# A list of 2,766 steps written anew: the issue order of a fused mLSTM and rational feed-forward kernel

## The chip, the cores and the metric

One core of a Trainium2 chip runs the whole program. The time is device time in microseconds (us) of one execution, and the profile shows the instructions of one such execution on the five engines: PE (TensorE), DVE (VectorE), ACT (ScalarE), POOL (GpSimd) and SP (SyncE), which here issues nearly all transfers. PEld is PE's weight load, which runs beside its matmuls.

## The reference

What is computed, cut to what matters (B=4, H=8, S=768, D=40; the feed-forward has 320 inputs, 2048 hidden columns and 3072 tokens):

```python
for t in range(S):                       # mLSTM, for every batch b and head h
    m_new = np.maximum(f_gate[:, :, t] + m, i_gate[:, :, t])
    f_stab = np.exp(f_gate[:, :, t] + m - m_new)
    i_stab = np.exp(i_gate[:, :, t] - m_new)
    m = m_new
    C = f_stab[..., None, None] * C + i_stab[..., None, None] * np.einsum('bhd,bhe->bhde', vt, kt)
    n = f_stab[..., None] * n + i_stab[..., None] * kt
    h_tilde = np.einsum('bhde,bhe->bhd', C, qt)
    denom = np.maximum(np.abs(np.einsum('bhd,bhd->bh', n, qt)[:, :, None]), 1.0)
    y[:, :, t] = sigmoid(o_gate[:, :, t]) * h_tilde / denom

x = y.transpose(0, 2, 1, 3).reshape(B * S, H * D)
h = x @ w_in
P = a[0] + a[1] * h + a[2] * h**2 + a[3] * h**3
Q = 1.0 + abs(b[0]) * abs(h) + abs(b[1]) * h**2
out = (P / (Q + 1e-06)) @ w_out
```

## The kernel before

The recurrence is worked in 24 units (`attention`, L841): a unit is 128 time steps of one batch with its 8 heads. Two units make a pair (`outputs`, L1056), whose result is 256 tokens of feed-forward input. The feed-forward (`feed_forward`, L1196) takes the tokens in 12 blocks of 256, and each block in 8 steps of 256 hidden columns, so there are 96 steps, named by block and step (`f2_0_3` is block 0, step 3). The weights arrive as raw 64-bit words and are split once, at the start, into a high and a low part (`split64`, L729), in 18 pieces: `i0` to `i7` and `j0`, `j1` of w_in, `o0` to `o7` of w_out.

Nothing is scheduled when the program is built. Every piece of work is put into a plan with its engine and with what it reads and writes (`_Plan.add`, L66), and the string `ORDER` (L145) then lists all steps by name, in one sequence for all engines and for the SP queue. `listed` (L89) reads it and `issue` (L114) issues the steps in that sequence. Each engine runs its own steps strictly in that order (`_Queue`, L22, ties each instruction to the one before it on its queue, and its line 34 is the one that nearly all instructions show in the profile). A buffer is handed out when its step is issued, so the order also decides which work waits for which buffer. A step's dot is its count: `s1_o7.1` is the second half of `s1_o7`.

The names that the order and the prediction use:

- Gates. `early` (L490) is the chain on DVE that makes the gate terms of the first 256 time steps; its last three steps on DVE are `early.17` (the exponentials, tile g), `early.20` and `early.21` (a scan that makes the running products a). `gate.5` to `gate.25` (`gates`, L565) do the same for the other 512 time steps, with four subtractions `lx` on DVE and four `li` on POOL; their tile is gate_x.
- Weight pieces. `raw` is the load; `s0`, `s2` and `o0` run on ACT, `s1` (tiles lo0, lo1) and `s3` (tile z) on DVE, `o2` (tiles wi, wo, wY) on POOL.
- Units. `pf`, `pa`, `tk`, `tq`, `S`, `ow` on PE (tiles fb, pa, kq, kq, ps, ow), `sc` (a scan, tile e), `qa`, `P`, `u0`, `u1` on DVE, `kp`, `ke`, `d0`, `d1` on POOL, `ek`, `eq` on ACT. Pairs: `it`, `i1` and the transpose `xt` on PE (tiles y, px), `rc`, `x`, `xl` on DVE (tiles na, xn, xk), `ab`, `xh` on ACT, `g` on POOL. `og` is the sigmoid of the output gate on ACT, which needs another activation table than `y`.
- A feed-forward step. `f1` on PE (16 matmuls into ph, in two halves), `ha`, `p1`, `u` on ACT, `p3` on DVE, `w` on POOL, `y`, `r0` on ACT, `gh` on DVE (tile gH), `f2` on PE (8 matmuls from gH into po), `m` on DVE (w<-w,gH), `rm` on POOL (p<-p,w), `gl` on DVE (tile gL), `f3` on PE (4 matmuls from gL). The last step, 11_7, is done in two halves.
- `hot` (90, at the start) and `hz` (24, at the end) are matmuls without use, which keep PE's clock up.

Of the kernel before, what the change touches and what calls it, by code (L numbers as in the profile page):

```python
# [150 lines left out]
s1_i0 o0_o1 tk_0 ek_0 raw_i6 s0_o5 s2_o5 s3_i4 o2_o1 s3_i0 li o0_i4 lx.1 lk_1 gate.3 s0_o7.1 lx o2_i4 s2_o7 o0_i0
s1_i3 raw_o3 s1_o5 hot.23 hot.24 hot.25 s1_o7.1 hot.26 hot.27 hot.28 hot.29 hot.30 hot.31 hot.32 hot.33 hot.34
hot.35 hot.36 hot.37 hot.38 hot.39 hot.40 hot.41 s2_i3 li.1 tq_0 lx.3 ke_0 s3_o7.1 zero s3_o5 s0_i6 s0_o7 s1_o7 eq_0
o2_i0 zero.11 gate.7 s0_o5.1 s3_o7 o0_o7 kp_1 s1_i6 s3_i3 hot.42 s2_i6 o2_o7 hot.43 hot.44 hot.45 raw_j0 hot.46
hot.47 hot.48 hot.49 hot.50 hot.51 hot.52 hot.53 hot.54 hot.55 pa_0 o0_i3 S_0 gate.8 gate.21 s1_o5.1 s3_i6 s3_o5.1
pc_0 qa_0 gate.9 o2_i3 s0_o3.1 P_0 lq_1 lk_2 hot.56 hot.57 hot.58 hot.59 tk_1 o0_i6 o2_i6 s0_o3 s2_o3 zero.5 zero.8
s1_o3 s1_o3.1 s3_o3 lv_0 raw_o0 ek_1 o0_o5 ogl_0 pf_1 s3_o3.1 lv_1 hot.60 hot.61 hot.62 hot.63 hot.64 s0_j0 s2_j0
sc_1 raw_i1 o0_o3 ogl_1 tq_1 raw_i2 eq_1 s1_j0 hot.65 gate.10 ow_0 pa_1 pc_1 pa_2 ke_1 o2_o3 zero.6 s0_o0.1 o2_o5
s3_j0 S_1 squares pc_2 qa_1 P_1 u0_0 ow_1 s2_o0 d1_0 hot.66 lk_3 raw_i5 lq_2 s1_o0.1 u0_1 hot.67 s0_o0 o0_j0 o2_j0
hot.68 hot.69 hot.70 hot.71 hot.72 hot.73 hot.74 hot.75 hot.76 s2_i1 s0_i1 u1_0 og_0 s3_o0.1 s1_o0 s1_i1 d1_1 raw_j1  # L160
s3_o0 it_0 i1_0 hot.77 hot.78 hot.79 ab_0 o0_o0 u1_1 s3_i1 pf_2 gate.11 sc_2 kp_2 tk_2 o2_j0.1 hot.80 s0_i2 it_0.1
rc_0 g_0 i1_0.1 ek_2 s2_i2 raw_o2 gate.12 s1_i2 ab_0.1 s0_i5 rc_0.1 gate.18 hot.81 x_0 hot.82 s3_i2 tq_2 hot.83
zero.9 ke_2 s1_i5 lv_2 hot.84 g_0.1 x_0.1 hot.85 gate zero.7 o0_i1 eq_2 hot.86 hot.87 pa_3 lq_3 oc_j0 raw_o4 lk_4
qa_2 o2_i1 s0_j1 s1_j1 xt_0 hot.88 xt_0.1 s2_i5 hot.89 pc_3 s3_i5 o2_o0 xh_0 s2_j1 o0_i2 xl_0 kp_3 s3_j1 ow_2 o0_i5
o2_i5 S_2 gate.1 tk_3 s0_o2.1 s0_o2 gate.13 u0_2 s1_o2 s2_o2 xh_0.1 s1_o2.1 d1_2 raw_o6 s3_o2 gate.14 raw_i7 u1_2
s3_o2.1 ek_3 xl_0.1 tq_3 o2_i2 o0_j1 s0_o4.1 eq_3 s0_o4 s2_o4 pf_3 P_2 f1_0_0 f1_0_0.1 o2_j1 gate.15 sc_3 gate.16
lv_3 lf_4 s1_o4.1 ke_3 kp_4 S_3 oc_j1 gate.19 s1_o4 s3_o4.1 s3_o4 ha_0_0 p1_0_0 s0_i7 f1_0_1 p3_0_0 P_3 u_0_0 lq_4
s1_i7 gate.17 o2_j1.1 s2_i7 o0_o4 ow_3 f1_0_1.1 s3_i7 w_0_0 s0_o6 o2_o4 y_0_0 ha_0_1 o0_i7 f1_0_2 f1_0_2.1 r0_0_0
lk_5 u0_3 gate.20 ogl_2 d1_3 qa_3 o2_i7 f1_0_3 gh_0_0 m_0_0 s1_o6 u_0_1 ha_0_2 w_0_1 p1_0_1 f2_0_0 f1_0_3.1 f2_0_0.1
p3_0_1 s2_o6 p1_0_2 u_0_2 s3_o6 it_1 i1_1 u1_3 p3_0_2 y_0_1 s0_o6.1 o0_o2 rm_0_0 gl_0_0 r0_0_1 w_0_2 o2_o2 ogl_3  # L170
ogl_4 la_4 f3_0_0 ogl_5 gate.22 y_0_2 s1_o6.1 s3_o6.1 ha_0_3 gh_0_1 m_0_1 r0_0_2 ab_1 gate.23 gate.24 f3_0_0.1
it_1.1 i1_1.1 p1_0_3 ab_1.1 f2_0_1 rc_1 d0_4 gh_0_2 rm_0_1 m_0_2 rm_0_2 lv_4 f1_0_4 f2_0_1.1 gl_0_1 og_2 u_0_3 g_1
f1_0_4.1 p3_0_3 f3_0_1 f3_0_1.1 tk_4 f2_0_2 ek_4 f2_0_2.1 ha_0_4 p1_0_4 u_0_4 sc_4 w_0_3 gl_0_2 tq_4 f3_0_2 y_0_3
r0_0_3 x_1 rc_1.1 g_1.1 f3_0_2.1 p3_0_4 w_0_4 la_5 lv_5 x_1.1 f1_0_5 f1_0_5.1 ha_0_5 gh_0_3 lq_5 lf_5 m_0_3 xt_1
f1_0_6 xh_1 y_0_4 r0_0_4 la_6 ke_4 kp_5 gate.32 xl_1 f2_0_3 f2_0_3.1 f1_0_6.1 f1_0_7 f1_0_7.1 p1_0_5 gh_0_4 eq_4
u_0_5 m_0_4 o0_o6 rm_0_3 rm_0_4 ha_0_6 gl_0_3 qa_4 f3_0_3 xt_1.1 xh_1.1 w_0_5 f3_0_3.1 gate.25 gl_0_4 ow_4 S_4 u_0_6
p3_0_5 xl_1.1 zero.10 o2_o6 u0_4 P_4 p1_0_6 y_0_5 f2_0_4 r0_0_5 w_0_6 f1_1_0 d1_4 gh_0_5 m_0_5 f2_0_4.1 f3_0_4 tk_5
rm_0_5 ha_0_7 u_0_7 p3_0_6 w_0_7 ek_5 p1_0_7 u1_4 sc_5 f3_0_4.1 f1_1_0.1 y_0_6 ha_1_0 r0_0_6 gl_0_5 p3_0_7 gh_0_6
tq_5 f2_0_5 eq_5 f1_1_1 f1_1_1.1 f2_0_5.1 p1_1_0 qa_5 u_1_0 ke_5 d0_5 lk_6 gate.28 lq_6 lq_7 la_7 S_5 m_0_6 y_0_7
ha_1_1 r0_0_7 P_5 ow_5 f3_0_5 f3_0_5.1 p3_1_0 w_1_0 y_1_0 gh_0_7 m_0_7 f1_1_2 rm_0_6 rm_0_7 f2_0_6 ogl_8 gate.29  # L180
ogl_6 lf_6 gl_0_6 u_1_1 u0_5 w_1_1 f1_1_2.1 d1_5 p1_1_1 r0_1_0 gl_0_7 f2_0_6.1 f3_0_6 f3_0_6.1 f2_0_7 f2_0_7.1
gh_1_0 m_1_0 p3_1_1 f3_0_7 ha_1_2 p1_1_2 u1_5 p3_1_2 f3_0_7.1 it_2 i1_2 it_2.1 i1_2.1 lv_6 ev_0_7 u_1_2 ev_0_7.1
kp_6 y_1_1 ab_2 rc_2 sc_6 tk_6 rm_1_0 d0_6 g_2 r0_1_1 w_1_2 ke_6 f2_1_0 f2_1_0.1 lk_7 ab_2.1 ek_6 gh_1_1 gl_1_0
y_1_2 r0_1_2 x_2 m_1_1 rc_2.1 f1_1_3 f1_1_3.1 gate.26 tq_6 ha_1_3 p1_1_3 rm_1_1 gh_1_2 m_1_2 g_2.1 rm_1_2 f3_1_0
eq_6 gl_1_1 p3_1_3 u_1_3 f1_1_4 f1_1_4.1 ha_1_4 u_1_4 w_1_3 lv_7 x_2.1 qa_6 f3_1_0.1 f2_1_1 f2_1_1.1 gl_1_2 kp_7 S_6
# [1245 lines left out]
```

## Time and profile before

| | |
|---|---|
| three runs, us | 532.27, 532.53, 533.85 (median 532.53) |
| profiled execution: span from first to last instruction | 527.5 us (its own time is not listed apart; the median is 5.0 us above the span) |
| busy share of the span | PE 95%, PEld 91%, DVE 85%, ACT 81%, POOL 73% |
| mean granted TensorE clock | 0.989 of full speed |
| chain that ended last, by engine | PE 76%, DVE 9%, ACT 5%, issue 3%, POOL 2%, DMA 2%, SP's queue 2% |
| moved by DMA | 42.46 MB, mean 80 GB/s, most of it in the first 70 us |

A share of busy time is a mean over stages. PE counts as busy from the start of a matmul to its modelled end, and these ends overlap, so PE can read as fully busy while it issues matmuls with gaps; how far apart the matmuls start tells more. The views below are cut by stage: the start up to 84 us, the change-over up to 96 us, the long body up to 514 us, and the end.

### The profile page before, as it was taken

Reading aid. Unit: us, or ns where it says so; the run is one execution under the profiler, and the core shown is the slowest. Engines: PE = TensorE matmul, PEld = TensorE weight load, DVE = VectorE, ACT = ScalarE, POOL = GpSimd, SP = SyncE. Lnnn points to the kernel's source line nnn. Section 1 sums busy time; section 2 is a strip of 40 time slices with the busy share of each in tenths; the row PEclk is TensorE's granted clock in tenths of the full one; section 3 lists DMA queues with packets and bytes.
Section 4 is the critical chain, followed back from the end, with each engine's and each line's share of the span. In section 5 each row is a group of like instructions: output and inputs, shape, how many; then the busy total and the mean of one; then the engine's idle time right before and its main releaser. Section 6 shows DMA issues by size and latency. Waiting matters only on the chain.

```text
span 527.5 us, 12998 instructions
## 1 busy us (share of the span) xinstructions
...
## 2 busy tenths in 40 slices
...
GB/s 189 279 171 207 246 72 126 47 77 125 77 132 126 60 49 24 149 30 116 139 14 2 134 29 111 69 23 69 78 15 2 99 43 1 2 26 1 26 1 32
DMA packets 119113, 42.46 MB, mean 80 GB/s; under 512 B 103554, under 2 KB 111810, under 8 KB 119042
## 3 DMA queue, kind: packets, MB, share of 16 engines
...
q10 hardware_dynamic: 130, 0.16, 0.1%
...
## 4 chain that ended last, share of the span: by engine, by line
PE 76%; DVE 9%; ACT 5%; issue 3%; POOL 2%; DMA 2%; SPq 2%; DVEq 0%; ACTq 0%
PE ph L34 30%; PE po L34 29%; PE y L34 4%; PE ps L34 4%; PE kq L34 3%; PE ow L34 2%; ACT ph L34 2%; SPq L34 2%; PE px L34 1%; DVE gH L34 1%; DVE gate_x L34 1%; DMA rawo<-in_moe_w_out_dram 1%; PE hot L34 1%; DMA qn<-in_q_dram 1%; DVE gL L34 1%
## 5 line engine op out<-in xcount | busy, mean ns | idle before, releaser
L34 POOL TENSOR_TENSOR p<-p,w 128x512 f32<-128x512 f32 (+1 forms) x97 | 129.2, 1332 | 81.1 <-DVE w L34 77.1
L34 PE MATMUL ph<-xk,wi 128*128 128x256 f32 x1152 | 170.5, 284 | 3.0 <-DVE xk L34 1.3
L34 PEld LDWEIGHTS ph<-xk,wi 128*128 128x128 f32 x1152 | 152.6, 188 | 4.8 <-DVE xk L34 1.7
L34 POOL TENSOR_TENSOR w<-w,ha 128x512 f32<-128x512 f32 (+1 forms) x97 | 129.5, 1338 | 13.1 <-ACT w L34 10.6
L34 PE MATMUL po<-wo,gH 128*128 128x320 f32 x768 | 137.4, 314 | 1.1 <-DVE gH L34 1.0
L34 PEld LDWEIGHTS po<-wo,gH 128*128 128x128 f32 x768 | 115.5, 188 | 3.5 <-DVE gH L34 1.9
L34 DVE SCALAR_TENSOR_TENSOR gH<-p,ps,ph 128x512 fp32r<-128x512 f32 (+1 forms) x97 | 71.4, 737 | 19.3 <-ACT ph L34 14.5
L34 DVE SCALAR_TENSOR_TENSOR gL<-p,ps,ph 128x512 fp32r<-128x512 f32 (+1 forms) x97 | 71.3, 736 | 17.7 <-POOL p L34 16.4
L34 ACT ACTIVATE ph<-w,cd 128x512 f32<-128x512 f32 (+1 forms) x97 | 66.4, 685 | 20.5 <-POOL w L34 11.3
L34 PE MATMUL po<-wo,gL 128*128 128x320 f32 x384 | 80.9, 318 | 1.8 <-DVE gL L34 1.8
L34 ACT ACTIVATE w<-ha,ba 128x512 f32<-128x512 f32 (+1 forms) x97 | 78.5, 811 | 3.9 <-POOL p L34 1.0
L34 DVE SCALAR_TENSOR_TENSOR w<-w,gH 128x512 f32<-128x512 f32 (+1 forms) x97 | 77.1, 794 | 4.4
L34 DVE SCALAR_TENSOR_TENSOR p<-p,ps,ph 128x512 f32<-128x512 f32 (+1 forms) x97 | 70.8, 735 | 6.1 <-ACT p L34 4.9
L34 ACT ACTIVATE ha<-ph 128x512 f32<-128x512 f32 (+1 forms) x97 | 57.2, 590 | 21.6 <-PE ph L34 21.0
L34 ACT ACTIVATE p<-ph,ps 128x512 f32<-128x512 f32 (+1 forms) x97 | 65.5, 676 | 3.1 <-DVE gL L34 3.0
L34 PEld LDWEIGHTS po<-wo,gL 128*128 128x128 f32 x384 | 59.1, 188 | 4.1 <-DVE gL L34 2.5
L34 ACT ACTIVATE ph<-ph 128x512 f32<-128x512 f32 (+1 forms) x97 | 56.2, 580 | 2.2
L34 PE MATMUL ph<-xk,wj 128*128 128x256 f32 x192 | 54.2, 282 | 0.0
L34 PE MATMUL ph<-xk,wY 128*128 128x256 f32 x192 | 54.1, 282 | 0.0
L34 PEld LDWEIGHTS ph<-xk,wj 128*128 128x128 f32 x192 | 36.2, 189 | 0.0
L34 PEld LDWEIGHTS ph<-xk,wY 128*128 128x128 f32 x192 | 36.2, 189 | 0.0
L34 PE MATMUL hot<-ident 128*128 128x128 f32 x180 | 26.1, 301 | 4.0 <-DVE flag_out L374 4.0
...
## 6 DMA issues: line engine op xcount, KB each, us to landing
...
```

The lines of the kernel that those rows point to most:

```text
L34: made = fn(*args, **kwargs)
```

## The change

Only the string `ORDER` is replaced: the same 2,766 steps stand in another sequence, derived by a program that is not part of the kernel and that now counts, operation by operation, that DVE and POOL exclude one another. No function, size, buffer count or instruction of the program is touched. Three lines of the old string fewer make all later line numbers smaller by 3. The diff, cut to its first lines:

```diff
 ORDER = """
-zero.2 zero.4 early early.1 raw_i0 s0_i0 gate.2 raw_o1 s0_o1 s0_o1.1 s2_o1 eye1 le early.2 early.3 early.4 early.5
-mc early.6 early.7 early.8 early.9 early.10 early.11 early.12 early.13 early.14 early.15 early.16 early.17 gate.4
-early.20 early.21 gate.5 li.2 hot hot.1 hot.2 hot.3 hot.4 hot.5 hot.6 hot.7 hot.8 hot.9 s1_o1 early.18 early.19
...
+zero.2 early early.1 le early.2 early.3 eye1 hot early.4 mc early.5 hot.1 hot.2 hot.3 hot.4 hot.5 hot.6 hot.7 hot.8
+hot.9 hot.10 hot.11 hot.12 hot.13 hot.14 hot.15 hot.16 raw_o1 s0_o1.1 zero early.6 early.7 gate.2 early.8 early.9
+gate.4 early.10 early.11 early.12 s1_o1.1 s0_o1 s2_o1 early.13 s1_o1 early.14 s3_o1 early.15 early.16 raw_i3 s0_i3 eye
...
```

Place one, DVE just after the first gate terms (g). Before, in a row (the scan g<-g,early_qA is `early.21`; gate_m is `gate.5`; lo and zo are pieces of the first weights):

```order
L34 SCALAR_TENSOR_TENSOR g_64<-early_qA_159,early_kT_158 128x128
L34 COPY gate_m_154<-cd_59 32x1
L34 MEMSET gate_f_155 128x128
L34 COPY early_qA_159<-g_64 128x1
L34 MEMSET g_64 128x1
L34 SCALAR_TENSOR_TENSOR g_64<-g_64,early_qA_159 128x64
L34 SCALAR_TENSOR_TENSOR gate_m_154<-gate_f_155,cd_59 32x512
L34 SCALAR_TENSOR_TENSOR lo0o1_175<-rawo1_173,lo0o1_175 128x320
```

and now:

```order
L34 SCALAR_TENSOR_TENSOR g_64<-early_qA_159,early_kT_158 128x128
L34 SCALAR_TENSOR_TENSOR zo1_218<-zo1_218,lo1o1_200 128x320
L34 COPY early_qA_159<-g_64 128x1
L34 MEMSET g_64 128x1
L34 SCALAR_TENSOR_TENSOR lo1o7_240<-rawo7_236,lo1o7_240 128x320
L34 SCALAR_TENSOR_TENSOR g_64<-g_64,early_qA_159 128x64
L34 SCALAR_TENSOR_TENSOR lo0i3_228<-rawi3_226,lo0i3_228 128x512
L34 SCALAR_TENSOR_TENSOR lo0o7_238<-rawo7_236,lo0o7_238 128x320
```

Work on weight piece o1 now stands within the gate chain, and work on piece o7, the third weight load of SP's queue, stands ahead of the scan; `gate.5` moved behind.

Place two, DVE between the first pair's result (xn) and its last step ahead of the feed-forward (xk, second half, `xl_0.1`). Before, the second half of that stretch:

```order
L34 SCALAR_TENSOR_TENSOR gate_x_156<-gate_x_156 128x256
L34 COPY sm0_136<-ow_2_830 40x4x41 x2
L34 SCALAR_TENSOR_TENSOR lo0o2_860<-rawo2_732,lo0o2_860 128x320
L34 SCALAR_TENSOR_TENSOR lo1o2_858<-rawo2_732,lo1o2_858 128x320
L34 SCALAR_TENSOR_TENSOR zo2_866<-zo2_866,lo0o2_860 128x320
L34 SCALAR_TENSOR_TENSOR gate_x_156<-gate_x_156 128x256
L34 TENSOR_TENSOR st2_132<-tm2_1_871,ow_2_830 40x4x41 x2
L34 SCALAR_TENSOR_TENSOR zo2_866<-zo2_866,lo1o2_858 128x320
L34 TENSOR_TENSOR xk0_819<-px1_0_808,xk0_819 128x2x128
L34 TENSOR_TENSOR xk0_819<-px1_0_808,xk0_819 64x128
```

and now:

```order
L34 TENSOR_TENSOR xn0_639<-y1_0_605,gt0_1_676 128x4x2x40
L34 SCALAR_TENSOR_TENSOR zo0_649<-zo0_649,lo0o0_664 128x320
L34 SCALAR_TENSOR_TENSOR lo0j1_671<-rawj1_565,lo0j1_671 128x512
L34 SCALAR_TENSOR_TENSOR lo0i5_690<-rawi5_560,lo0i5_690 128x512
L34 SCALAR_TENSOR_TENSOR zj1_693<-zj1_693,lo0j1_671 128x512
L34 SCALAR_TENSOR_TENSOR lo0i1_698<-rawi1_568,lo0i1_698 128x512
L34 TENSOR_TENSOR xk0_718<-px0_0_714,xk0_718 128x2x128
L34 TENSOR_TENSOR xk0_718<-px0_0_714,xk0_718 64x128
L34 SCALAR_TENSOR_TENSOR zi5_754<-zi5_754,lo0i5_690 128x512
L34 TENSOR_TENSOR xk0_718<-px1_0_724,xk0_718 128x2x128
```

Of the 103 steps that DVE ran up to `xl_0.1`, 21 now follow it: all of `gate.8` to `gate.14`, `gate.18`, `gate.21`, the work on piece o2, parts of i1 and i2, and unit 2's `sc`, `qa`, `u0`, `u1`.

Place three, ACT in blocks 1 and 2 of the feed-forward, where two groups of sigmoids (og3 with og4, og5 with og6) are made. Before, the second group has its own pair of table loads:

```order
L34 ACT_TABLE_LOAD
L34 ACTIVATE og5_2146<-og5_2146 128x640
L34 ACTIVATE og6_1955<-og6_1955 128x640
L34 ACTIVATE ha2_4_2509<-ph2_4_2430 128x512
L34 ACTIVATE w2_4_2512<-ha2_4_2509,ba_124 128x512
L34 ACTIVATE p2_4_2517<-ph2_4_2430,ps_123 128x512
L34 ACT_TABLE_LOAD
```

and now both groups stand between one pair:

```order
L34 ACT_TABLE_LOAD
L34 ACTIVATE og5_1623<-og5_1623 128x640
L34 ACTIVATE og6_1413<-og6_1413 128x640
L34 ACTIVATE w1_7_2076<-ha1_7_2005,ba_124 128x512
L34 ACTIVATE ha2_0_2100<-ph2_0_2079 128x512
L34 ACTIVATE w2_0_2102<-ha2_0_2100,ba_124 128x512
L34 ACTIVATE p2_0_2104<-ph2_0_2079,ps_123 128x512
L34 ACTIVATE og3_1882<-og3_1882 128x640
L34 ACTIVATE og4_1893<-og4_1893 128x640
L34 ACTIVATE y0_3_2124<-y0_3_2124 128x8
L34 ACT_TABLE_LOAD
```

So the executed branch has 13 table loads in place of 15.

## Rows read from the trace of the kernel before

**Rows 1.** Busy time of the engines in eight stretches of the span. Columns: stretch in us, its length, then busy us and instructions of PE, PEld, DVE, ACT and POOL, the granted TensorE clock, the DMA share and GB/s.

```profile
4.00:24.00 20.00, 17.07 (x146) 16.70 (x147) 18.36 (x47) 12.21 (x22) 9.57 (x19) 0.91 0.96 286
24.00:44.00 20.00, 16.97 (x275) 15.51 (x273) 19.56 (x43) 16.12 (x29) 15.07 (x16) 0.91 0.90 193
44.00:64.00 20.00, 15.67 (x239) 13.68 (x234) 19.61 (x44) 17.95 (x37) 14.44 (x17) 1.00 0.96 231
64.00:84.00 20.00, 17.47 (x171) 16.15 (x172) 18.98 (x36) 19.48 (x34) 17.15 (x14) 1.00 0.49 85
84.00:96.00 12.00, 11.52 (x110) 10.95 (x109) 9.57 (x21) 11.81 (x22) 10.05 (x11) 1.00 0.47 87
96.00:130.00 34.00, 34.00 (x346) 33.04 (x345) 32.20 (x56) 27.45 (x50) 30.85 (x28) 1.00 0.49 94
...
150.00:180.00 30.00, 28.93 (x289) 26.97 (x289) 25.61 (x44) 25.92 (x47) 22.40 (x20) 1.00 0.45 96
180.00:514.00 334.00, 332.94 (x3130) 323.89 (x3127) 283.84 (x474) 276.88 (x487) 246.78 (x220) 1.00 0.24 51
```

**Rows 2.** The chain of work that ended last, in order of time, from 83 to 115 us (start us, us, engine and tile): where it passes from DVE and ACT to PE, and what PE's groups cost there when it is dense.

```profile
83.61 0.40 DVE xn L34
...
93.61 0.70 PE ow L34 x16
...
100.52 1.90 PE ph L34 x16
...
113.81 1.19 PE po L34 x8
```

**Rows 3.** DVE in order of time, the gate steps and two of the first `m` (start us, us, engine, line, operation, out<-in and shape, count).

```profile
17.30 1.54 DVE L34 TENSOR_TENSOR gate_x<-gate_f,gate_m 32x128 f32<-32x128 f32 x1
...
20.80 0.28 DVE L34 TENSOR_TENSOR gate_x<-gate_f,gate_m 32x128 f32<-32x128 f32 x1
...
21.11 1.27 DVE L34 TENSOR_TENSOR gate_x<-gate_f,gate_m 32x128 f32<-32x128 f32 x1
...
23.81 1.09 DVE L34 TENSOR_TENSOR gate_x<-gate_f,gate_m 32x128 f32<-32x128 f32 x1
...
28.26 1.62 DVE L34 TENSOR_SCALAR gate_x<-gate_x 128x256 f32<-128x256 f32 x1
...
32.94 0.28 DVE L34 TENSOR_SCALAR gate_x<-gate_x 128x256 f32<-128x256 f32 x1
...
54.42 0.42 DVE L34 SCALAR_TENSOR_TENSOR gate_x<-gate_x 128x256 f32<-128x256 f32 x1
...
56.79 1.39 DVE L34 SCALAR_TENSOR_TENSOR gate_x<-gate_x 128x256 f32<-128x256 f32 x1
...
70.68 1.80 DVE L34 SCALAR_TENSOR_TENSOR w<-w,gH 128x512 f32<-128x512 f32 x1
...
79.82 0.69 DVE L34 SCALAR_TENSOR_TENSOR w<-w,gH 128x512 f32<-128x512 f32 x1
```

**Rows 4.** POOL in order of time, the one instruction beside the gate step of 28.26 us (columns as in rows 3; in brackets the idle time before it and what ended it).

```profile
28.19 1.54 POOL L34 TENSOR_TENSOR wo<-zo,wo 128x640 fp32r<-128x640 f32 x1 [0.78 <-ACT wo L34]
```

**Rows 5.** DVE in order of time again: the scan `early.21`, the first and the last of the eleven steps that leave the stretch ahead of step 2's gL (`gate.16` and unit 4's `sc`), the two longest waits between 84 and 96 us, and the second `xl` of a pair.

```profile
11.15 0.29 DVE L34 TENSOR_TENSOR_SCAN g<-g,early_qA 128x64 f32<-128x64 f32 x1
...
62.05 0.40 DVE L34 SCALAR_TENSOR_TENSOR gate_x<-gate_x 128x256 f32<-128x256 f32 x1
...
81.75 1.23 DVE L34 TENSOR_TENSOR_SCAN e<-fb,eye 128x512 f32<-128x512 f32 x1
...
85.45 0.49 DVE L34 TENSOR_TENSOR xn<-y,gt 128x320 f32<-128x320 f32 x1 [0.46 <-POOL gt L34]
...
87.56 0.75 DVE L34 SCALAR_TENSOR_TENSOR gH<-p,ps,ph 128x512 fp32r<-128x512 f32 x1 [1.62 <-ACT ph L34]
...
94.14 0.73 DVE L34 TENSOR_TENSOR xk<-px,xk 128x256 fp32r<-128x256 f32 x2
```

**Rows 6.** DVE's groups of the whole span, by form (busy us and mean ns of one behind the bar, then the idle time before them).

```profile
L34 DVE TENSOR_TENSOR pm<-ps,e 128x512 f32<-128x512 f32 x24 | 16.5, 687 | 2.2 <-PE ps L34 1.9
...
L34 DVE TENSOR_TENSOR_SCAN e<-g,eye 128x512 f32<-128x512 f32 x10 | 15.6, 1558 | 0.1
...
L34 DVE TENSOR_TENSOR st<-tm,ow 40x164 f32<-40x164 f32 x48 | 15.3, 319 | 2.6 <-POOL tm L34 1.9
```

**Rows 7.** ACT in order of time, the first work on the second and the third weight piece that landed (columns as in rows 3).

```profile
11.54 0.46 ACT L34 ACTIVATE lo0o<-rawo 128x320 int32<-128x320 uint8 x1 [2.64 <-DMA rawo<-in_moe_w_out_dram]
...
14.00 0.62 ACT L34 ACTIVATE lo0i<-rawi 128x512 int32<-128x512 uint8 x1
```

**Rows 8.** ACT in order of time: a table load in block 2 and the instruction behind it.

```profile
144.50 1.28 ACT L34 ACT_TABLE_LOAD   x1
145.79 0.69 ACT L34 ACTIVATE ph<-w,cd 128x512 f32<-128x512 f32 x1
```

**Rows 9.** The chain that ended last, from 505 us on (columns as in rows 2): the halved last step, from its first ACT work to PE's last useful matmuls.

```profile
505.20 0.40 ACT ha L34
...
513.39 2.61 PE po L34 x16
```

**Rows 10.** ACT in order of time in the same stretch, between the second half's ha and its w.

```profile
506.46 0.46 ACT L34 ACTIVATE p<-ph,ps 128x256 f32<-128x256 f32 x1
...
508.03 0.59 ACT L34 ACTIVATE w<-ha,ba 128x256 f32<-128x256 f32 x1
```

More of the change, by code (lines that the diff above doesn't have):

```diff
@@ L151 @@
[L151 to L185, printed above, removed]
@@ L311 @@
-f3half_11_7.1 hz.9 hz.10 hz.11 ev_11_7 ed_11_7 ev_11_7.1 hz.12 hz.13 hz.14 hz.15 hz.16 hz.17 hz.18 hz.19 hz.20 hz.21
-hz.22 hz.23
+zero.2 early early.1 le early.2 early.3 eye1 hot early.4 mc early.5 hot.1 hot.2 hot.3 hot.4 hot.5 hot.6 hot.7 hot.8
+hot.9 hot.10 hot.11 hot.12 hot.13 hot.14 hot.15 hot.16 raw_o1 s0_o1.1 zero early.6 early.7 gate.2 early.8 early.9
+gate.4 early.10 early.11 early.12 s1_o1.1 s0_o1 s2_o1 early.13 s1_o1 early.14 s3_o1 early.15 early.16 raw_i3 s0_i3 eye
+s2_i3 ogl_0 raw_o7 s0_o7 s0_o7.1 hot.17 hot.18 hot.19 hot.20 hot.21 hot.22 early.17 early.18 early.19 zero.9 zero.1
@@ new lines @@
+zero.5 hot.23 hot.24 hot.25 hot.26 hot.27 hot.28 lk_0 kp_0 tk_0 s3_o1.1 o0_o1 s2_o7 o2_o1 zero.4 early.20 s1_o7.1
+early.21 pa_0 s1_i3 s1_o7 s3_i3 s3_o7 s3_o7.1 ek_0 o0_i3 o2_i3 raw_o3 s0_o3.1 raw_i6 lq_0 gate.3 lk_1 pc_0 s2_o3 s0_i6
+s0_o3 gate.5 li.1 li.3 zero.7 pf_0 sc_0 ke_0 kp_1 o0_o7 pa_1 pc_1 o2_o7 hot.29 hot.30 tq_0 hot.31 eq_0 hot.32 hot.33
+pf_1 s2_i6 raw_i4 raw_i0 raw_j0 ogl_1 lq_1 lk_2 lv_0 raw_o5 gate.6 s1_o3.1 s1_o3 s3_o3.1 s3_o3 s0_i4 lx.2 s1_i6 lx.1
+s3_i6 o0_o3 o0_i6 o2_i6 qa_0 S_0 hot.34 hot.35 hot.36 hot.37 s0_i0 P_0 s1_i4 s2_i0 hot.38 tk_1 ek_1 hot.39 hot.40
@@ new lines @@
+hot.41 hot.42 hot.43 s1_i0 s3_i0 sc_1 lx s0_j0 s2_i4 s3_i4 lx.3 tq_1 hot.44 o0_i0 eq_1 qa_1 s1_j0 hot.45 hot.46 pa_2
+pc_2 ow_0 li.2 o2_o3 li zero.6 zero.3 u0_0 S_1 ke_1 P_1 lv_1 ow_1 u0_1 hot.47 hot.48 raw_i5 raw_o0 lq_2 raw_j1 raw_i1
+o2_i0 o0_i4 s2_j0 og_0 s0_o5 d1_0 u1_0 s3_j0 o2_i4 kp_2 s1_o5 s2_o5 it_0 i1_0 ab_0 rc_0 it_0.1 i1_0.1 hot.49 hot.50
+hot.51 hot.52 hot.53 hot.54 hot.55 hot.56 hot.57 hot.58 s0_o5.1 s1_o5.1 s3_o5 d1_1 u1_1 s3_o5.1 g_0 x_0 lv_2 raw_i2
+raw_i7 gate.1 s2_o0 o0_j0 raw_o2 oc_j0 gate zero.11 ab_0.1 rc_0.1 s0_o0 s0_o0.1 s1_o0.1 o0_o5 s0_j1 gate.7 s3_o0.1
@@ new lines @@
+s1_o0 g_0.1 x_0.1 s3_o0 s1_j1 hot.59 tk_2 ek_2 hot.60 s0_i5 s1_i5 s2_j1 s3_j1 o2_o5 o2_j0 s0_i1 s1_i1 o0_o0 o2_o0
+o2_j0.1 hot.61 hot.62 hot.63 hot.64 hot.65 hot.66 hot.67 hot.68 hot.69 xt_0 xh_0 xl_0 hot.70 xt_0.1 hot.71 hot.72
+hot.73 hot.74 hot.75 hot.76 pf_2 hot.77 hot.78 hot.79 s2_i5 s3_i5 raw_o6 lq_3 lk_3 raw_o4 xh_0.1 o0_j1 o2_j1 oc_j1
+zero.8 xl_0.1 sc_2 s0_i2 s1_i2 s2_i2 o0_i5 s2_i1 o2_i5 gate.21 s3_i1 s3_i2 ke_2 tq_2 eq_2 f1_0_0 hot.80 hot.81 s0_i7
+o0_i1 zero.10 o2_i1 f1_0_0.1 hot.82 hot.83 S_2 hot.84 hot.85 hot.86 hot.87 kp_3 o0_i2 o2_i2 s0_o2 qa_2 gate.8 squares
```

272 lines of the change are left out of this document (145 added, 127 removed).

## The prediction

> **What bounds the kernel now.** I read the stretches first, then the chain that ended last, then the timelines of DVE, POOL and ACT where these pointed. The stretches show three stages. From 4 to 84 us DVE is busy 18.36 + 19.56 + 19.61 + 18.98 = 76.5 of 80 us; PE's figure there says little, as much of its work is the useless `hot` [rows 1]. From 96 us on PE never rests: 34.00 of 34.00 us, then 332.94 of 334 [rows 1]. The chain agrees: it runs over DVE, POOL and ACT up to the gH at 88 us and over matmuls afterwards [rows 2, 5]. So the end time is the time at which PE becomes dense, plus the PE work then left, plus PE's later gaps, plus the tail. An order cannot make PE's work smaller; it can make PE dense earlier (a matter of DVE), close gaps, or shorten the tail.
>
> A dense PE also hides small gaps in "busy", and PEld shows them: its share is 323.89/334 = 0.970 from 180 us on but 26.97/30 = 0.899 from 150 to 180 us, which is 0.071 x 30 = 2.1 us short [rows 1].
>
> Exclusion is to be seen in the timelines. The same gate_x step on 32x128 takes 0.28 us once and 1.54, 1.27 and 1.09 us the other times; a TENSOR_SCALAR on 128x256 takes 0.28 or 1.62; a SCALAR_TENSOR_TENSOR 0.42 or 1.39; the first `m` 1.80 where a free one takes 0.69 [rows 3]. The step of 28.26 us ends at 29.88, right behind POOL's instruction from 28.19 to 29.73 [rows 3, 4].
>
> **The change part by part.** Only the sequence moves, so I weigh at fixed points of PE's work what DVE must have done ahead of it, old list against new, at the old durations.
>
> *The start of the feed-forward.* DVE's last step ahead of the first `f1` now is the 82nd, where it was the 103rd; the 21 steps that left the stretch cost about 15 us. None is saved: they follow later. Hence this is worth nothing by itself, and the later points count.
>
> *Point one, step 2's gL in block 0.* Eleven DVE steps leave the stretch ahead of it, the first at 62.05 (0.40), the last at 81.75 (1.23), 5.9 us together [rows 5]; step 3's gH and `m` enter it (0.75 and 0.69, 1.4 us) [rows 3, 5]. DVE: -4.5 us. PE has one half of an `f1` more behind it, 8 matmuls, 1.90/2 = 0.95 us [rows 2]. Together 5.4 us ahead.
>
> *Point two, step 4's gL.* DVE has 1.3 us fewer gate work, but `P` (0.69), the second `xl` (0.73), step 5's `p3` (as long as a gH, 0.75) and unit 5's `sc` (1.23) more: +2.1 us [rows 5, 6]. PE has half an `f1` more (0.95), and two groups of transposes for one `ow` (0.70), which I set against each other [rows 2]. Before, DVE waited here 0.46 + 1.62 = 2.1 us [rows 5], and a DVE that is late would not wait. Together 2.1 - 2.1 + 0.95 = 1.0 us ahead.
>
> *Point three, step 3's gL in block 1.* DVE: +0.5 us (unit 7's scan at the 1.56 us mean of its kind or above and a `p3` against four state updates of 2 x 0.32 us a pair, an `m` and a scan) [rows 3, 6]. PE: 2.6 us less behind it (a whole `f1`, 1.9, and an `ow`, 0.7) [rows 2]. DVE's idle time in the old run up to there is 12 - 9.57 + 34 - 32.20 = 4.2 us [rows 1]. Together 4.2 - 0.5 - 2.6 = 1.1 us ahead.
>
> PE's density is set by the tightest point, so 1.0 us.
>
> *A wait that is added.* The merge of lo1o7, from the third weight load, now stands ahead of `early.21`, which ran at 11.15 us [rows 5]. Four half-merges of piece o1 (0.4 each) come ahead of it too, so DVE is free at about 12.8 us. The second weight piece was first touched at 11.54 us, when its transfer released ACT, and the third at 14.00 [rows 7]. After 14.0 come two ACT steps of 0.46 us, then the merge can begin, at about 15: DVE stands for about 2.3 us. Queued behind it are `early.21`, the work on i3 and o7 and `gate.5`; waiting for the scan are `pa` on PE and all of unit 0 behind that. The loss lies on DVE, the bound of this stage, so I count it in full; its bounds are 0 (the transfer comes earlier, as PE's and ACT's chains have room) and 2.3.
>
> *Exclusion avoided.* What the rows above lost up to 84 us is 1.26 + 0.99 + 0.81 for the three 32x128 steps, 1.34 + 0.97 for the two 128x256 ones, and 1.11 for the `m`: 6.5 us [rows 3]. The new list places `lx.2` and `lx.1` after one POOL weight step and ahead of the next, which looks like an escape, but POOL is busy 17.15 of 20 us from 64 to 84 [rows 1], where most of the gate steps now go. I take half, 3.2 us; the bounds are 0 and 6.5.
>
> First the rows: a step of either engine that finds the other one inside such an instruction waits for its end [rows 3, 4]. The Trainium skill, "SBUF — State Buffer", section "Who interferes with whom", says that the engine which issues first holds the shared port pair for its whole instruction and the other blocks fully. The trace agrees with it in the step of 1.62 us. By that rule a list only chooses who pays, as far as POOL has no free time; that is the second rival below.
>
> Start, summed: 1.0 - 2.3 + 3.2 = 1.9 us sooner; bounds -1.3 and 7.5.
>
> *The body.* Of the 2.1 us that PEld is short from 150 to 180 us [rows 1], the cover was lost where POOL and ACT ran late; the new list has two table loads fewer just ahead of and in it, 2 x 1.28 = 2.6 us of ACT [rows 8]. I take 1.5 us as closed. The bounds are 2.1 closed, or none closed and a new gap of the same size elsewhere, for which the 2.1 us are the nearest row. ACT's next instruction starts at 145.79, 0.01 us behind the load's end [rows 8]: no more than the load is lost. The Trainium skill, "ScalarE: Activation LUTs", section "What ACT_TABLE_LOAD costs", adds a drain of about 1.38 us to each switch; by it ACT would save 5.3 us in place of 2.6, the whole gap would close, and the sum would be 0.6 us better. The trace shows no such drain.
>
> *The tail.* From the halved step's first ACT work at 505.20 to PE's last useful matmul at 516.00 are 10.8 us [rows 9], in which PE's other work does not fill the time. In the new list one `f3` and one `f2` that stood behind the last `f1` now stand ahead of it: 4 matmuls and 8, 12 x 0.147 = 1.8 us by the 1.19 us that 8 po matmuls take in dense work [rows 2]. If the chain stays as long, the end is 1.8 us later against PE's work. But on ACT the second half's `u` now follows its `ha` at once, where `p1`, `y` and `r0` stood between 506.46 and 508.03: 1.6 us shorter [rows 10]. I take zero; the bounds are 1.8 worse and 1.6 better.
>
> Sum: 1.9 + 1.5 + 0 = 3.4 us off. The span would be 527.5 - 3.4 = 524.1 us; the median of the runs is 5.0 us above the profiled span, so 529.1, which I give as **529.0 us**.
>
> **The rivals.** *VectorE starved and late (slower).* The order brings POOL's and DVE's work apart on paper only, the wait for the third load costs its 2.3 us, and the tightest point gives back 1.0: the start is 1.3 us late. DVE then runs closer to PE in block 1 (point three has PE 2.6 us behind), and one gap of the size of that at 150 us, 2.1 us, is added. 532.5 + 1.3 + 2.1 = 535.9 us. It decides when less than 1.3 us of the 6.5 is escaped. For it: DVE has only 3.5 us to spare of 80 [rows 1]. Against it: POOL has 5.6 free us from 44 to 64 [rows 1], room for some escapes.
>
> *The lock only changes its payer (no change).* DVE escapes 1.3 to 2 us net, as POOL waits where DVE did and its late `o2`, `w` and `rm` are waited for in turn; the gap in the body stays. 1.0 - 2.3 + 1.3 to 2 is 0 to 0.7: 531.8 to 532.5 us.
>
> *All of it (more than forecast).* 6.5 us escaped, no wait at the start, the body's gap closed: 1.0 + 6.5 + 1.5 = 9.0 us, 523.5 us. Against it: POOL's load from 64 to 84 us [rows 1].
>
> **How the numbers follow.** About 0.3%, 1.6 us, is what a measurement of this kernel can tell from no change: faster is below 530.9 us, slower above 534.1. Chances: the forecast (527 to 530.9) 0.42, all of it 0.16, the lock changing its payer 0.18, starved 0.24. So faster 0.58, same 0.18, slower 0.24. The best ends together give 7.5 + 2.1 + 1.6 = 11.2 us, 521.3; the worst 1.3 + 2.1 + 1.8 = 5.2 us, 537.7. Both at once are unlikely, so the range is 522.0 to 536.5 us.
>
> **What would show it.** In the profile of the changed kernel: the first ph matmul well before 60 us; a DVE wait of about 2 us for ACT's lo1o at 13 to 15 us; the gate_x steps mostly near 0.28 and 0.42 us, and the mean of w<-w,gH below its old one; PE dense some 2 us sooner measured in PE work, so that the first output stores come sooner; 13 table loads; PEld's share from 150 to 180 us nearer 0.97. Wrong it would be if DVE, no longer the bound, gives way to ACT in the start (18 to 19.5 of 20 us from 44 to 84 [rows 1]), if the gate steps moved past 84 us stretch POOL's `w` and `rm` and PE waits for gL, or if a transfer that now comes later in SP's queue (piece i0, or i1 and i2) holds the feed-forward's first steps.

## The result and the profile after

Fifteen runs of the changed kernel have a median of 534.97 us (533.37 to 536.53), fifteen of the kernel before 532.27 us (529.66 to 533.85). The ratio is 1.0059 with an interval of 1.0043 to 1.0075: about 3 us slower, where 3.4 us faster was forecast. The time lies within the stated range of 522.0 to 536.5 us, but above the time of the kernel before and not below it.

First a correction of the base. The profiled execution of the changed kernel took 533.61 us at a span of 531.7, 1.9 us above its span. By the same 1.9 the profile of before, at 527.5, is of an execution of some 529.4 us (an estimate), just below the lowest of its fifteen runs, 529.66. So the 5.0 us that the prediction put between span and median were 1.9 us around the span and about 3 of luck. The profiles therefore tell where time goes, and the timed runs how much.

The stretches of the changed kernel, columns as in [rows 1]:

```profile
4.00:24.00 20.00, 17.09 (x222) 16.04 (x223) 17.60 (x51) 14.03 (x27) 11.40 (x20) 1.00 1.03 263
24.00:44.00 20.00, 15.36 (x199) 14.23 (x200) 16.61 (x36) 15.21 (x28) 14.46 (x17) 0.91 1.02 211
44.00:64.00 20.00, 17.87 (x237) 16.74 (x236) 18.34 (x42) 18.74 (x35) 15.98 (x16) 1.00 0.90 228
64.00:84.00 20.00, 19.64 (x201) 18.50 (x200) 19.68 (x40) 19.76 (x36) 17.81 (x16) 1.00 0.45 84
84.00:96.00 12.00, 11.87 (x111) 11.33 (x112) 11.28 (x21) 11.50 (x22) 11.25 (x9) 1.00 0.68 129
96.00:130.00 34.00, 32.48 (x327) 30.85 (x322) 32.47 (x56) 27.64 (x53) 25.92 (x24) 1.00 0.53 89
150.00:180.00 30.00, 29.88 (x313) 28.64 (x311) 25.46 (x47) 22.01 (x42) 22.05 (x22) 1.00 0.38 82
180.00:514.00 334.00, 326.82 (x3048) 317.38 (x3047) 278.11 (x462) 271.13 (x479) 242.06 (x214) 0.99 0.23 51
```

Up to 84 us DVE is now busy 72.2 of 80 us (76.5 before), and PE is fuller from 64 to 96 us; from 96 to 130 it is busy 32.48 of 34 us, where it had 34.00. From 150 to 180 us PEld has 28.64 of 30 us, where it had 26.97. But from 180 us on PE is busy 326.82 us, where it was 332.94: the loss is in the long body, the stretch in which the old kernel hardly stood.

A sum over PE's matmuls says the same in one column. I take the useful matmuls that have started up to a time at the usual distance between two starts of their kind (0.1195 us for ph, 0.147 for po, 0.035 for ow and y, and so on, medians of the trace of before) and subtract that work from the time. What is left is the time that PE has lost so far; each row is of one profiled execution:

| lost up to, us | 110 | 180 | 250 | 300 | 500 | last useful matmul |
|---|---|---|---|---|---|---|
| before | 28.0 | 32.6 | 35.7 | 38.1 | 41.9 | 45.4 |
| changed | 25.6 | 29.0 | 31.5 | 37.6 | 43.8 | 49.6 |

The changed order leads by 4.2 us at 250 us, has 0.5 of that left at 300, is 1.9 behind at 500 and 4.2 at the end. Two places stand out.

**Block 5, at 273 us.** PE in order of time (start us, us, then line, operation, tiles, in brackets the idle time before and what ended it):

```profile
273.03 0.31 PE L34 MATMUL y<-sm,qA 104*64 104x82 f32 x4
275.89 1.65 PE L34 MATMUL ph<-xk,wi 128*128 128x256 f32 x6 [2.55 <-DVE st L34]
```

The `f1` of step 5_3 waits 2.55 us for a step on DVE that it has no use for: `u1_15` (tile st). All PSUM tiles but `po` share six banks, handed out in the order of the list, and this `f1` got the bank that `u1_15` frees. DVE in the same stretch, then POOL:

```profile
268.87 1.89 DVE L34 SCALAR_TENSOR_TENSOR w<-w,gH 128x512 f32<-128x512 f32 x1
...
272.76 2.50 DVE L34 TENSOR_TENSOR_SCAN e<-fb,eye 128x512 f32<-128x512 f32 x1
275.19 0.65 DVE L34 TENSOR_TENSOR st<-tm,ow 40x164 f32<-40x164 f32 x2
```

```profile
268.94 1.28 POOL L34 TENSOR_TENSOR w<-w,ha 128x512 f32<-128x512 f32 x1
...
272.90 1.26 POOL L34 TENSOR_TENSOR p<-p,w 128x512 f32<-128x512 f32 x1
```

Two instructions of DVE started 0.07 and 0.14 us ahead of one of POOL and took 1.89 and 2.50 us in place of 0.69 and 1.23 [rows 3, 5]: 2.5 us of exclusion in the list that counts it. And ACT, which PE's next banks need too:

```profile
268.15 0.67 ACT L34 ACTIVATE p<-ph,ps 128x512 f32<-128x512 f32 x1
272.92 1.28 ACT L34 ACT_TABLE_LOAD   x1 [4.10 <-DVE p L34]
```

Behind the gap PE works at half its clock (columns of the stretches as above, PEclk third from the end):

```profile
272.00:275.90 3.90, 1.35 (x39) 1.18 (x35) 3.80 (x6) 2.97 (x5) 3.57 (x3) 0.93 0.01 4
275.90:278.70 2.80, 2.80 (x13) 2.80 (x14) 2.55 (x4) 2.32 (x5) 1.27 (x2) 0.50 0.47 86
```

The granted clock is 0.50, which is 1.2 in place of 2.4 GHz, for 2.8 us, so a part of the gap is paid for again: lost time grows from 32.7 us at 270 to 37.3 at 280, by 4.6 us for a gap of 2.55.

**The tail.** PE again:

```profile
506.47 1.34 PE L34 MATMUL po<-wo,gH 128*128 128x320 f32 x8
510.71 1.56 PE L34 MATMUL ph<-xk,wi 128*128 128x256 f32 x6 [2.91 <-DVE p L34]
...
512.50 1.27 PE L34 MATMUL po<-wo,gL 128*128 128x320 f32 x4
```

The second half of the last `f1` stands 2.91 us for DVE's `p3` of the first half, although it reads nothing of it, and again the clock falls:

```profile
507.80:510.70 2.90, 0.00 (x1) 0.00 (x0) 2.69 (x5) 1.08 (x3) 2.27 (x3) 1.00 0.00 0
510.70:514.20 3.50, 3.48 (x15) 3.49 (x16) 0.62 (x1) 1.35 (x3) 1.28 (x2) 0.52 0.00 0
```

### The profile page after: what moved, and what is told of

Read it like the earlier page. It is cut to its first block, busy times and chain, and to the rows that moved or that the text cites. A ratio compares the mean times of both kernels' runs of the same rounds, so it can differ in the third digit from the quotient of the medians.

```text
span 531.7 us, 12964 instructions
## 1 busy us (share of the span) xinstructions
PE 501.8 (94%) x4943; PEld 483.1 (91%) x4943; DVE 444.1 (84%) x798; ACT 421.5 (79%) x750; POOL 382.2 (72%) x360
## 4 chain that ended last, share of the span: by engine, by line
PE 48%; DVE 19%; POOL 12%; issue 7%; ACT 7%; DMA 4%; SPq 1%; DVEq 0%; POOLq 0%; ACTq 0%
PE ph L34 19%; PE po L34 18%; POOL p L34 4%; POOL w L34 3%; DVE gH L34 3%; PE y L34 3%; DVE w L34 3%; ACT ph L34 2%; PE ps L34 2%; DVE p L34 2%; DVE gL L34 2%; PE kq L34 2%; PE ow L34 2%; DVE e L34 1%; DMA qn<-in_q_dram 1%
## 5 line engine op out<-in xcount | busy, mean ns | idle before, releaser
L34 PE MATMUL ph<-xk,wi 128*128 128x256 f32 x1152 | 172.7, 286 | 6.2 <-DVE p L34 2.9
L34 POOL TENSOR_TENSOR w<-w,ha 128x512 f32<-128x512 f32 (+1 forms) x97 | 127.1, 1312 | 15.6 <-ACT w L34 14.8
L34 DVE SCALAR_TENSOR_TENSOR w<-w,gH 128x512 f32<-128x512 f32 (+1 forms) x97 | 75.9, 783 | 3.5
L34 ACT COPY qb<-kq 40x512 f32<-40x512 f32 x48 | 27.9, 580 | 3.0 <-PE kq L34 2.8
```

The source lines that it names most:

```text
L34: made = fn(*args, **kwargs)
```

## The experiments

All kernels differ from the changed one in `ORDER` alone. The changed order is cut in three: the start, its first 1,216 steps (up to about 222 us), the middle, steps 1,217 to 2,612 (to about 475 us), and the tail. Where a part is taken from the other list, the steps already issued are left out of the rest. Ratios are to the kernel before, timed in the same rounds (its medians 531.2 to 531.9); the rounds ran on several chips, so between rounds ratios say more than medians.

**1. The new start alone** (new_start): changed steps 1 to 1,216, all others as before.

> The first 1,216 steps of the changed order (up to about 222 us), then all others in the order of before. Theory A: the start and the blocks up to there are worth what the trace shows, 3.7 us less PE time lost at 222 us, and nothing in the old order behind it takes them back: 532.3 - 3.7 = 528.6 us, ratio to before 0.993, table loads 13 or 14. Theory B (a start that is ahead only runs into VectorE sooner): the gain is gone by 320 us as in the changed kernel, 531.5 to 532.5, ratio 0.999 to 1.000.

527.57 us, ratio 0.9917 (0.9895 to 0.9938): 3.3 to 5.6 us faster than before. PE's lost time goes from 34.8 at 250 us to 41.0 at 500 and 44.4 at the end, as fast as in the kernel before (35.7, 41.9 and 45.4). Theory A holds by the timed runs; the start is a clear gain, and the loss must lie behind it. The profiles alone would not have shown it: at 250 us this one is only 0.9 us below that of before, which was a fortunate execution.

**2. The new middle alone** (new_middle): start and tail as before.

> The kernel before with its middle alone in the new order: steps 1,217 to 2,612 (some 222 to 475 us), start and tail in the old order. Theory A (the middle of the new order is worse by itself: PE loses 12.3 us from 250 to 500 us there against 6.2 with the old one): about 5 us slower than before, 536 to 537 us, ratio 1.008 to 1.012. Theory B (it is worse only because the new start brings PE's work forward, closer to a DVE that does not keep up): with the old start it costs under 2 us, ratio under 1.004.

540.56 us, ratio 1.0175 (1.0150 to 1.0200), worse than either theory. PE's wait at `f1_5_3` is there again, 2.5 us, the clock behind it too; lost time grows by 4.7 us from 280 to 290. New gaps of 0.1 to 0.5 us lie behind the seam at 222 to 236 us, where an old start meets a list that reckons with a DVE further on. So the middle is worse by itself. What it costs differs with what stands ahead of it: 0.0175 x 532 = 9.3 us here, with the new one 5.5 us by the medians and 6.4 by the ratios (experiment 3 against 1: 533.05 - 527.57, and 1.0038 - 0.9917 of 532). How much of the 9.3 is the seam was not tried.

**3. The new order with the old tail** (old_tail).

> The first 2,612 steps of the changed order (up to the second step of block 11, some 475 us), the rest in the order of before. It tells what the new tail alone costs: by the traces PE's lost time grows by 5.8 us from 500 us to the end in the changed kernel and by 3.5 in the kernel before. Theory A (three places, independent): 2.3 us sooner than the changed kernel, 532.7 us, ratio to before about 1.002. Theory B (a late DVE in the body hands its delay on to the tail, whatever its order): under 0.7 us, 534.5 to 535.

533.05 us, ratio 1.0038 (1.0016 to 1.0060) against 1.0059: the new tail costs 1.1 us by the ratios and 1.9 by the medians, and the intervals overlap. From 500 us to the end the lost time grew by 5.8 us in the changed kernel, by 3.5 in the kernel before and by 3.4 here (45.7 to 49.1). It leans to theory A; experiment 8 adds to it.

**4. Old steps around 273 us** (old_270): steps 1,217 to 1,660 of the middle as before, its rest and the tail new.

> The changed order with steps 1,217 to 1,660 (some 222 to 297 us) in the order of before; the later body and the tail stay in the new order. Theory A (most of what the new body costs lies at the one place at 273 us, with the fall of the clock behind it): PE's lost time grows from 220 to 300 us by about 3.7 us in place of 6.9, the kernel takes 531 to 532.5 us; the stalls at 371 to 376 and 454 us (0.7 us each) remain. Theory B (the losses are spread): 534 to 535.

530.91 us, ratio 1.0009 (0.9987 to 1.0031): some 3 of the middle's 5.5 to 6.4 us lie in this stretch by the ratios, 4 by the medians. Lost time grows from 31.9 at 220 us to 35.6 at 300, by the 3.7 that were expected.

**5. One step at 273 us, first try** (u1_first):

```diff
-r0_5_1 ev_4_7.1 sc_16 d1_15 u1_15 gh_5_1
+r0_5_1 ev_4_7.1 d1_15 u1_15 sc_16 gh_5_1
```

> The changed order with one step moved: unit 16's scan sc stands behind unit 15's state update u1 on DVE, in place of ahead of it. Theory A (one bank, one place): PE's 2.55 us at 273.3 us is the wait of f1_5_3 for the bank that u1_15 frees; u1_15 then ends at about 273.7 us in place of 275.84, PE waits some 0.3 us, its clock stays at 1.00 behind it, and of the 4.6 us lost there 2.5 to 4.5 return: 530.5 to 532.5 us. Theory B (DVE starved): what DVE owes there is only paid one step later, under 1 us sooner, 534 to 535.

535.58 us, ratio 1.0073 (1.0053 to 1.0093): no gain. The wait for the bank did shrink, and the rest of it went two steps on:

```profile
279.55 0.99 PE L34 MATMUL ph<-xk,wi 128*128 128x256 f32 x6 [0.38 <-DVE st L34]
...
284.00 0.62 PE L34 MATMUL kq<-ident,kp 128*104 128x128 f32 x4 [0.68 <-DVE gL L34]
```

By the timed runs theory B was right here: the bank is only where DVE's lateness shows. The profile is less clear: the clock stayed at 1.00 in it, and from 250 to 320 us it lost 1.6 us less than that of the changed kernel. Why the runs show nothing of this is open. (The start of this profile was a late one, below.)

**6. One step at 273 us, second try** (p3_first):

```diff
-P_15 gh_5_0 m_5_0 u1_14 u0_15 f2_4_7 ... it_7.1 p1_5_1 p3_5_1 w_5_1
+P_15 gh_5_0 p1_5_1 p3_5_1 m_5_0 u1_14 u0_15 f2_4_7 ... it_7.1 w_5_1
```

> The changed order with block 5's p1_5_1 and p3_5_1 moved ahead of m_5_0, which on DVE is the instruction of 1.89 us that POOL's w_5_1 stretches. ACT's idle 4.10 us at 268.8 us ends with p3_5_1. Theory A (the chain through p3 sets the place): ACT's table load and y_5_1 start some 1.5 to 2.5 us sooner, PE's wait for the bank shrinks from 2.55 us to 1 to 1.5 and the clock stays at 1.00: 1 to 3 us sooner, 532 to 534 us. Theory B (DVE's queue as a whole is late there, in whatever order): the wait keeps its length, within 0.7 us of the changed kernel.

531.50 us, ratio 1.0004 (0.9986 to 1.0022): about 3 us off (0.0055 of 532) by moving one step of DVE and its feeder. ACT, then PE, then the stretch behind the gap:

```profile
268.43 1.28 ACT L34 ACT_TABLE_LOAD   x1 [0.86 <-DVE p L34]
```

```profile
273.37 0.98 PE L34 MATMUL ph<-xk,wi 128*128 128x256 f32 x6 [1.28 <-DVE st L34]
```

```profile
273.30:276.00 2.70, 2.63 (x21) 2.64 (x22) 2.63 (x5) 0.90 (x3) 2.07 (x3) 1.00 0.12 20
```

ACT idles 0.86 in place of 4.10 us, the scan runs in 1.23 us as POOL now works elsewhere, PE's gap is 1.28 us and the clock does not fall. The cause at 273 us is thus the place of `p3_5_1` behind a stretched `m_5_0` and two state updates, which held ACT, POOL's next steps and the banks. The one edit ended ACT's wait, the stretching of the scan and the fall of the clock together; what each of them was worth by itself was not tried.

**7. The tail's f1 two steps earlier** (tail_early):

```diff
-f1half_11_7 f2_11_4 f2_11_4.1 rm_11_4 ... p3half_11_7 rm_11_6 f1half_11_7.1 hahalf_11_7.1
+f1half_11_7 f2_11_4 f2_11_4.1 f1half_11_7.1 rm_11_4 ... p3half_11_7 rm_11_6 hahalf_11_7.1
```

> The changed order with one step of the tail moved: the second half of the last step's f1 stands right behind f2_11_4 on PE, as it did before the change, in place of behind the first half's p3. Theory A (shared tile): the 2.9 us that PE stands at 507.8 us comes from the order alone, since the second half, issued behind the first half's p3, waits for this reader of the tile that both halves share; moved, it does not wait, PE's clock stays at 1.00 and the last useful matmul ends 2.5 to 3.7 us sooner: about 531.3 to 532.5 us, against 535.0 for the changed kernel. Theory B (DVE late in the tail anyway): the wait only moves to the next step, under 0.5 us sooner, 534.5 to 535.

535.77 us, ratio 1.0070 (1.0046 to 1.0095): no gain. The wait for `p3` is gone, so it did come from the order, but ACT's first `ha` now waits for the second half, and PE waits later:

```profile
507.76 0.69 ACT L34 ACTIVATE ph<-w,cd 128x512 f32<-128x512 f32 x1 [0.46 <-DVE p L34]
510.23 0.39 ACT L34 ACTIVATE ha<-ph 128x256 f32<-128x256 f32 x1 [1.77 <-PE ph L34]
```

```profile
514.41 0.85 PE L34 MATMUL po<-wo,gL 128*128 128x320 f32 x4 [1.79 <-DVE gL L34]
...
518.36 1.43 PE L34 MATMUL po<-wo,gL 128*128 128x320 f32 x4 [1.47 <-DVE gL L34]
```

The first half of `f1` had ended at 508.07 and `ha` needs only that. The tile ties its halves in both directions: whichever access is issued later waits for the earlier one.

**8. The tail's halves side by side** (tail_next): as 7, but right behind `f1half_11_7`.

> The changed order with the second half of the last f1 right behind the first half, as in the kernel before; all else of the new tail stays. In tail_early it stood two steps later, and ACT's first ha waited for it (1.78 us). Theory A (the halves are tied through their shared tile in both directions, so only side by side do they cost nothing): PE does not wait for p3, ACT's ha waits about 1 us less than in tail_early, and the tail loses 3.5 to 5 us from 500 us to the end in place of 5.8 and 7.0: 532.5 to 534.5 us. Theory B (the rest of the new tail's order, DVE's and ACT's, is what costs): as long as the changed kernel or longer, 535.

532.66 us, ratio 1.0019 (1.0001 to 1.0036), about 2 us off; lost time grows by 4.2 us in the tail in place of 5.8. Theory A.

**9. Useless matmuls in the tail's gap** (hz_in_gap): `hz` to `hz.11` ahead of `f1half_11_7.1`.

> The changed order with twelve of the 24 useless hz matmuls placed ahead of the second half of the last f1 on PE, where PE stands for 2.9 us. The wait itself stays. Theory A (the clock): the granted clock stays at 1.00 behind it, the eight matmuls take 1.1 us in place of 1.99 and the f3 and f2 behind them 0.45 and 0.75 each in place of 0.73 and up to 1.07, so that the last useful matmul ends 0.9 to 1.6 us sooner: 533.4 to 534.1 us against 535.0. Theory B: the matmuls are slow there for another reason (their weights or their tile), and nothing changes.

534.96 us, ratio 1.0064 (1.0042 to 1.0086): the time does not change. The clock theory is right in the trace all the same:

```profile
509.99 2.84 PE L34 MATMUL hz<-ident 128*128 128x128 f32 x24
513.07 0.97 PE L34 MATMUL ph<-xk,wi 128*128 128x256 f32 x6 [0.24 <-DVE p L34]
```

Six matmuls take 0.97 us where they took 1.56, at an unchanged wait for `p3`. A new wait of 1.15 us at `f3_11_6`, for DVE's gL, takes much of that back (the tail loses 5.0 us in place of 5.8), and timed runs do not resolve what is left.

**10. The loads of v** (lv_early): new_start with

```diff
-lq_1 lk_2 ... lv_0 ... raw_o5 ... lv_1
+lq_1 lv_0 lv_1 lk_2 ... raw_o5
```

> The order of new_start (start new, the rest old) with two loads moved in SP's queue: lv_0 and lv_1, the v of units 0 and 1, stand ahead of lk_2 in place of behind it and behind a piece of weights. Theory A (the new start hangs on this load): PE's ow_1, which stood 2.0 to 4.9 us for the transfer in the profiles of the new start, waits under 1 us, PE's work is 1.5 to 3 us further on at 110 us, and the runs scatter less: 524.5 to 526 us, against 527.6 for new_start. Theory B (the load is only the first of several that are late, next the weights j1 and i1 for the first f1): under 0.7 us sooner.

526.93 us, ratio 0.9904 (0.9888 to 0.9919), 0.6 us below new_start and inside its interval: theory B. The longest wait of PE from 30 to 46 us (us in total, times, longest), first in new_start, then in u1_first, which has the same start, then in this kernel:

```profile
PE ow L34 <- DMA vb<-in_v_dram: 3.6, 1, 3.6
```

```profile
PE ow L34 <- DMA vb<-in_v_dram: 4.9, 1, 4.9
```

```profile
PE px L34 <- DVE zo L34: 2.0, 1, 2.0
```

The wait for v is gone, and ACT waits 2.2 us for a weight piece instead: v is not the only transfer of the start that comes late.

**11. The transpose gate.22** (gate22): new_start with `gate.22` and `gate.23` behind `f2_0_6.1`.

> The order of new_start with gate.22 (a transpose on PE) and gate.23 (its copy on ACT) placed behind f2_0_6 in place of between the halves of f1_1_1. Theory A: PE's 1.4 us at 101 to 103 us, which are the wait for gate.20, a DVE step that POOL's o2_o6 stretches from 0.41 to 1.97 us, go, and nothing else is late: 526.0 to 526.6 us. Theory B (DVE's delay by the stretched step stays and the next step of PE pays): 527.2 to 527.6.

527.10 us, ratio 0.9912 (0.9899 to 0.9925): theory B. In its profile PE's wait of 1.27 us has become three: 0.84 us at `gate.22` in its new place, and 0.32 and 0.38 us at two other steps.

**12. Both of them** (both).

> The order of new_start with both of these edits, the loads lv_0 and lv_1 earlier and gate.22 later. If both theories A hold: 523.2 to 524.7 us, ratio to before 0.985 to 0.988; if neither: 527.5.

527.77 us, ratio 0.9923 (0.9904 to 0.9942): neither adds anything. The best kernels are 10, 11 and 1, which the intervals do not tell apart; they beat the kernel before by 0.8 to 1.0% and the changed one by about 1.4%.

**13. Both one-step repairs** (two_fixed): the changed order with the edits of 6 and 8.

> The changed order with both single-step repairs, that of p3_first (block 5's p1_5_1 and p3_5_1 ahead of m_5_0) and that of tail_next (the two halves of the last f1 side by side). Theory A (two independent places carry the loss): their gains add, 3.1 + 2.2 us off the changed kernel: 529 to 530.5 us, ratio to before 0.995 to 0.998, that is the new start's gain less what is left of the new body. Theory B (each repair alone only moved the wait within the same lateness of DVE, so that the second finds nothing left): no better than the better one of them, ratio 1.000 to 1.002.

531.06 us, ratio 0.9999 (0.9974 to 1.0024). Better than the changed kernel, but not told apart from either repair alone. In the profile they do add at their places: lost time grows from 33.6 at 260 us to 36.4 at 300, where tail_next alone has 33.6 to 39.0. In the tail PE's clock fell to 0.51 behind a gap of about 2 us, which it had not done behind the same gap in tail_next, and the tail lost 5.3 us, not 4.2. Whether the gains add in time stays open.

## Why the prediction was wrong

*The base.* "The median is 5.0 us above the profiled span" was taken for a constant. It is 1.9; the rest was one fortunate execution. This moves no term, but it hid that the start scatters: kernels whose start is the same, step for step, have between 24.0 (p3_first) and 30.6 us (u1_first) lost at 110 us in their profiles, and PE's `ow` of unit 1 waited 2.0 and 4.9 us for its v in these two.

*The start, 1.9 us with bounds -1.3 and 7.5: right in size.* Together with the gap at 150 to 180 us, 3.4 us were forecast; new_start measures 3.3 to 5.6. The added wait was put at 2.3 us, ending at about 15:

```profile
13.19 0.06 DVE L34 MEMSET g<- 128x1 f32 x1
14.96 0.49 DVE L34 SCALAR_TENSOR_TENSOR lo1o<-rawo,lo1o 128x320 int32<-128x320 int32 x1 [1.71 <-ACT lo1o L34]
```

It is 1.71. Exclusion escaped was put at 3.2 of 6.5 us; the same kinds of steps lose about 2.9 us in the new trace up to 84 us (1.40 of it in one), so some 3.6 escaped. What points one to three (1.0 us) are worth was not measured by itself. The two longest, on DVE and the POOL instructions beside them:

```profile
23.54 1.68 DVE L34 TENSOR_TENSOR gate_x<-gate_f,gate_m 32x128 f32<-32x128 f32 x1
...
98.49 1.97 DVE L34 SCALAR_TENSOR_TENSOR gate_x<-gate_x 128x256 f32<-128x256 f32 x1
```

```profile
23.52 1.55 POOL L34 TENSOR_TENSOR wo<-zo,wo 128x640 fp32r<-128x640 f32 x1
...
98.63 1.55 POOL L34 TENSOR_TENSOR wo<-zo,wo 128x640 fp32r<-128x640 f32 x1
```

The second is `gate.20`, moved out of the start. Behind it on DVE stands a state update (st, 100.39 us), and PE's `gate.22` stood 1.27 us until that ended; its tile pi is one of those that share the six banks. One sign of being wrong that the prediction named showed too: a transfer held the feed-forward's first steps, as PE's ph waited 1.6 us for the DMA of wj, and the kernel before has no such wait.

*The gap at 150 to 180 us, 1.5 of 2.1 us: right.* PEld is 0.955 of the stretch where it was 0.899; 0.055 x 30 = 1.7 us came back. There are 13 table loads.

*The body behind it, nothing: wrong, and this is the step that failed.* I walked the list up to block 2, where DVE is known to bound, and left the 330 us behind it as they were because PE "never rests" there [rows 1]. The only bound was "a new gap of the same size elsewhere", 2.1 us. The new middle costs 5.5 to 6.4 us, 3 to 4 of them at one place, where in the profile a gap of 2.55 us and the half clock behind it add up to 4.6. What else shows are idle waits of 0.2 to 0.5 us, one each at 316, 371, 374 and 454 us.

*The tail, zero with bounds 1.8 worse and 1.6 better: mis-sized.* It costs 1 to 2 us. I counted the matmuls that changed sides of the last `f1` and ACT's steps between its halves, and did not ask what a half waits for that is issued behind the first half's readers. That wait was 2.91 us.

*The rivals.* The starved VectorE gave 535.9 us, near the 534.97 measured, and it was right that exclusion would come back as one gap. But its place (the start late, a gap in block 1) was wrong: the start gained, and the gap came in block 5. The lock that only changes its payer did not hold, since the start keeps its gain. The Trainium skill's rule cited there ("SBUF — State Buffer", section "Who interferes with whom", that whoever issues first holds the shared port and the other blocks) agrees with the rows at 23.52 and 98.63 us only in part: at 23.52 POOL's started first and DVE's ended late, but at 98.49 DVE's instruction started ahead of POOL's by 0.14 us, by the recorded starts, and was still the one that ended late.
